# Linear attention and an MLP on one core: the keys' sum partly on VectorE, more warming matmuls, two denominators side by side, a new order

## The chip, the cores and the metric

The kernel runs on one core of a Trainium2 chip. The metric is device time in microseconds (us). Each run is one launch; the time before is the median of three.

## The reference

One transformer block with 2048 tokens of width 512 in bf16. What is computed, cut to the core:

```python
def _A_ref(x, wqkv, wo):                      # H = 32 heads of 16
    q, k, v = split(x @ wqkv)                 # each (heads, 2048, 16)
    phi = lambda t: jnp.where(t > 0, t + 1, jnp.exp(t)) + 1e-6
    pq, pk = phi(q), phi(k)
    kv  = jnp.einsum("bhsd,bhse->bhde", pk, v)
    z   = jnp.einsum("bhsd->bhd", pk)         # the keys' sum over all tokens
    num = jnp.einsum("bhqd,bhde->bhqe", pq, kv)
    den = jnp.einsum("bhqd,bhd->bhq", pq, z)[..., None] + 1e-6
    return merge_heads(num / den) @ wo
h  = x + _A_ref(_layernorm(x), A_wqkv, A_wo)
h2 = h + relu(_layernorm(h) @ B_w1) @ B_w2    # hidden width 1792
```

The second input `B_x` is not used.

## The kernel before

The tokens are 16 tiles of 128 rows (t = 0 to 15), and four chunks of 512 rows (c = 0 to 3); the width is four blocks of 128 columns (jb or kd = 0 to 3). All data stays on the chip. PSUM is one tile `bk` of eight banks, and the program assigns each bank by number.

The whole program is one string, `ORDER`. Each word is an operation with its indices: `K.8.0` calls `op_K(8, 0)`. The words are issued one after the other, and each goes to the queue of its engine, so on each engine the order of the words is the order of execution; semaphores between the engines follow from the tiles that are read and written. Nothing is reordered by a scheduler. An index list ends in a bank (TensorE), or in a count of neighbouring blocks (the others). All DMAs are issued by SyncE, in the order of the string, and a transposing DMA waits on that queue for its data.

The stages, with the words that the change and the prediction speak of:

- **Start.** `warm` issues matmuls of zeros into a bank that nobody reads (L233). `lx`, `lk`, `lq`, `lv`, `lo`, `l1`, `l2` load x and the weights wk, wq, wv, wo, w1, w2. For each tile `S` and `A` take mean and variance (VectorE, L236 and L237), `R` takes the reciprocal root as Ln and Exp (ScalarE, L242 and L243), `N` writes the normalised rows (VectorE, L250). They are transposed for tiles 0 to 5 on TensorE (`T`, L269) and copied out of PSUM by ScalarE or VectorE (`E`, `V`), and for tiles 6 to 15 by a transposing DMA (`X`, L290).
- **Keys.** `K` is x @ wk for a tile (four matmuls of 512 columns, L298). phi is Exp (`F`, ScalarE, L316), Relu (`U`, ScalarE, L319), min with 1 (`M`, VectorE, L323) and the sum of both (`D`, VectorE, L326). The keys lie in `pk`: tiles 0 and 1 in `pk_lo`, tile t from 2 on in slice t - 2 of `acts[0]`. `G` adds the outer product of normalised rows and keys for a tile into banks 4 to 7 (four matmuls, L350). `z` sums the keys over all tokens as matmuls of one column against ones (L358), one word for each block of 128 columns.
- **Attention's small matrices.** `gD` and `gA` copy G, `zc` and `zh` copy the keys' sum and spread it over heads, `kv`, `kx` and `m`, `mD` fold v's weights and wo into `m_sb`.
- **Queries.** `Q` (L306), `qF`, `qU`, `qM`, `qD` as for the keys, by chunk, into `pqT`.
- **Denominators.** `d4` gives the 32 heads' denominators for a chunk: four matmuls, each into 32 rows of one bank (L405). `dl4` and `dx4` make the reciprocals as Ln and Exp (ScalarE, L411 and L416) in `ld` and `rd`, which have two slots (c % 2). For chunk 0, `rp` spreads them by a matmul and `rm` multiplies; for the others `wb` writes them to DRAM, eight `rb` read them back spread over rows (L436), and `dm` multiplies (L443).
- **Second half.** `h` and `hD` give the attention's output plus x (L452, L458), `s`, `a`, `r`, `n` its layer norm, `t` or a DMA `x` its transposes, `p` (`ph` for half a chunk) the first layer of the MLP (L467, L476), `pA` and `pD` its Relu, `f` the second layer (L496), `fo` the result (L504) and `fd` its store.

The tile of zeros for the warming matmuls is a block of `m_sb`:

```python
zeros = m_sb[:, 0, :]
nc.vector.memset(zeros, 0.0)
```

Of the kernel before, what the change touches and what calls it, by code (L numbers as in the profile page):

```python
# [15 lines left out]


ORDER = """
table const masks warm.70.7.64 lx.0.1 S.0 lx.3.1 lx.2.1 lx.1.1 S.3 S.2 A.0 A.3 A.2 R.0.1 S.1 R.2.2 N.0.2.2 A.1
N.0.0.2 N.2 R.1.1 N.3 N.1 lk.0.2 lx.4.2 lk.2.2 T.0.3.2.2 warm.1.7 T.0.0.0.2 T.2.2 E.0.2.2 T.3.3 T.1.1 V.2  # L20
E.0.0.2 E.1 K.0.0 lx.6.2 S.4 E.3 S.5 A.5 A.4 F.0.1 R.4.2 U.0.1 S.7 S.6 M.0.1 N.4 K.2.2 K.1.1 F.1.1 U.1.1 K.3.3
D.0.1 A.6 A.7 R.6.2 M.1.1 N.5 lx.8.4 D.1.1 N.7 T.4.0 G.0 T.5.1 F.2.1 E.4 E.5 U.2.1 S.9 S.8 N.6 M.2.1 A.9 A.8
D.2.1 F.3.1 R.8.2 U.3.1 G.1 K.4.0 K.5.1 F.4.2 U.4.2 M.3.1 S.10 N.8 D.3.1 A.10 S.11 M.4.2 N.9 D.4.2 A.11
lx.12.4 lq.2.2 X.7 X.6 lv.0.2 R.10.2 G.2 K.7.3 G.3 K.6.2 F.6.2 U.6.2 lq.0.2 X.8 X.9 S.13 S.12 A.13 N.11 N.10
A.12 M.6.2 X.11 X.10 D.6.2 R.12.2 G.4 G.5 K.8.0 K.9.1 F.8.2 U.8.2 N.13 S.14 N.12 S.15 A.14 A.15 M.8.2 D.8.2
R.14.2 N.15 N.14 G.6 G.7 K.11.3 K.10.2 X.13 X.12 lo.2.2 X.14 X.15 l1.2.2 l2.0.7 lo.0.2 l1.0.2 lv.2.2 l2.7.7
F.10.2 U.10.2 G.8 G.9 K.12.0 K.13.1 U.12.2 F.12.2 M.10.2 D.10.2 M.12.2 G.10 K.14.2 K.15.3 Q.0.0.0 Q.0.1.1 G.11
F.14.2 U.14.2 M.14.2 D.12.2 G.12 D.14.2 qF.0.0.2 qU.0.0.2 G.13 z.1.2 G.14 Q.0.3.1 z.0.2 Q.0.2.0 G.15 z.2.2
z.3.2 qU.0.2.2 qF.0.2.2 gD.0.2 zc gA.2.2 qM.0.0.2 Q.1.1.3 Q.1.0.2 qF.1.0.2 qU.1.0.2 kv.1.4 kv.0.4 kv.3.4
kv.2.4 zh qM.0.2.2 qD.0.0.2 qD.0.2.2 kx Q.1.2.0 m.0.4 m.1.5 d4.0.3 m.3.7 m.2.6 Q.1.3.1 dl4.0 dx4.0 Q.2.1.3  # L30
qF.1.2.2 qU.1.2.2 qM.1.0.2 mD.0.2 mD.2.2 rp.0.0.4 rp.0.3.7 rp.0.1.5 rp.0.2.6 Q.2.0.2 qM.1.2.2 rm.0.0.2
rm.0.2.2 qD.1.0.2 qD.1.2.2 Q.2.3.1 Q.2.2.0 qU.2.0.2 qF.2.0.2 h.0.4 h.1.5 Q.3.0.2 Q.3.1.3 hD.0 hD.1 s.0 s.1 a.0
h.2.6 a.1 n.0 n.1 hD.2 qF.2.2.2 qU.2.2.2 h.3.7 t.0.4 qU.3.0.2 qF.3.0.2 e.0 Q.3.2.0 d4.1.4 t.1.5 Q.3.3.1 hD.3
s.2 s.3 a.2 a.3 n.2 n.3 v.1 t.2.6 dl4.1 dx4.1 qF.3.2.2 qU.3.2.2 v.2 t.3.7 wb.1 ph.0.1.3.0 ph.0.0.2.0 rb.1.0
rb.1.4 rb.1.2 rb.1.6 rb.1.1 rb.1.7 rb.1.5 rb.1.3 v.3 ph.0.1.3.1 ph.0.0.2.1 pD.0.0.2 qM.2.2.2 ph.0.3.1.1
ph.0.2.0.0 ph.0.2.0.1 ph.0.3.1.0 p.0.4.2 p.0.5.3 pA.0.2.2 p.0.6.0 p.0.7.1 pA.0.6.2 pD.0.4.2 p.0.8.2 p.0.9.3
p.0.11.1 p.0.10.0 pA.0.8.2 dm.1.0.2 dm.1.2.2 h.6.6 hD.6 h.5.5 p.0.13.3 h.7.7 hD.5 qM.3.0.2 s.6 a.6 s.5
qM.2.0.2 n.6 a.5 qD.2.2.2 h.4.4 hD.4 f.2.6.0.7 p.0.12.2 s.4 qD.2.0.2 qD.3.0.2 qM.3.2.2 hD.7 a.4 n.5 s.7 a.7
pA.0.10.2 pA.0.12.2 r.0.4 n.7 n.4 f.0.4.0.7 f.0.4.7.7 f.2.6.7.7 f.3.7.0.7 fo.0 x.5 x.4 x.6 fd.0 d4.2.4 dl4.2
dx4.2 x.7 wb.2 f.1.5.0.7 f.3.7.7.7 f.1.5.7.7 p.1.1.1 p.1.0.0 p.1.2.2 p.1.3.3 rb.2.6 rb.2.0 rb.2.4 rb.2.2  # L40
rb.2.7 rb.2.5 rb.2.3 rb.2.1 fo.3 pA.1.0.2 fo.1 fo.2 pA.1.2.2 dm.2.2.2 dm.2.0.2 p.1.4.0 p.1.5.1 p.1.6.2 p.1.7.3
r.4.4 pA.1.4.2 p.1.8.0 p.1.9.1 h.11.7 h.10.6 h.8.4 pD.1.8.2 pA.1.6.2 p.1.10.2 p.1.13.1 p.1.11.3 pA.1.10.2 hD.8
s.8 hD.11 h.9.5 p.1.12.0 f.4.4.0.7 pA.1.12.2 hD.10 s.10 f.4.4.7.7 f.7.7.0.7 hD.9 s.11 a.11 s.9 a.9 n.11 n.9
a.8 a.10 n.10 qD.3.2.2 fo.4 n.8 x.11 x.9 x.8 x.10 d4.3.4 dl4.3 dx4.3 wb.3 fd.1 f.6.6.0.7 f.5.5.0.7 f.6.6.7.7
p.2.0.0 p.2.3.3 p.2.2.2 p.2.1.1 pA.2.0.2 pD.2.2.2 fd.3 rb.3.6 rb.3.0 rb.3.7 rb.3.4 rb.3.2 rb.3.1 rb.3.5 rb.3.3
fd.4 fd.2 f.5.5.7.7 p.2.4.0 f.7.7.7.7 fo.5 p.2.7.3 p.2.6.2 p.2.5.1 pA.2.4.2 dm.3.2.2 fo.7 dm.3.0.2 h.12.4
h.13.5 hD.12 fo.6 pA.2.6.2 p.2.9.1 p.2.10.2 p.2.8.0 pD.2.8.2 r.8.4 p.2.11.3 h.15.7 p.2.12.0 p.2.13.1 pA.2.12.2
pA.2.10.2 h.14.6 f.8.4.0.7 s.12 hD.15 hD.13 s.13 a.13 hD.14 f.10.6.0.7 a.12 n.13 n.12 s.14 a.14 s.15 a.15 n.15
n.14 fd.5 fd.6 x.12 x.15 f.11.7.0.7 f.8.4.7.7 f.9.5.0.7 f.10.6.7.7 fo.8 fd.7 x.14 x.13 f.11.7.7.7 f.9.5.7.7
p.3.1.1 p.3.0.0 pA.3.0.2 p.3.2.2 p.3.3.3 p.3.5.1 p.3.4.0 fo.9 pA.3.4.2 fo.11 pD.3.2.2 fo.10 p.3.7.3 p.3.6.2  # L50
p.3.9.1 p.3.8.0 pD.3.6.2 pD.3.8.2 f.14.6.0.7 f.13.5.0.7 p.3.13.1 p.3.10.2 p.3.12.0 p.3.11.3 pA.3.12.2 r.12.4
pD.3.10.2 f.12.4.0.7 f.14.6.7.7 f.13.5.7.7 f.12.4.7.7 fd.10 fd.8 fd.9 fd.11 fo.13 fo.14 fo.12 fd.12 fd.14
fd.13 f.15.7.0.14.0.2 fo.15.0.2 fd.15.0.2 f.15.5.0.14.3.1 fo.15.3.1 fd.15.3.1 f.15.4.0.14.2.1 fo.15.2.1
fd.15.2.1
"""


# [1 line left out]
def kernel(  # L59
# [94 lines left out]
    def pk(t, n=1):  # L154
        return pk_lo[:, t : t + n, :] if t < 2 else acts[0][:, t - 2 : t - 2 + n, :]
# [22 lines left out]
        )  # L178

    def op_const():  # L180
        nc.vector.memset(zeros, 0.0)
# [2 lines left out]
        nc.vector.memset(ones[:], 1.0)
# [23 lines left out]
    def op_masks():  # L208
        op_mask()
        op_maskh()  # L210


    def op_gate():
        nc.gpsimd.memset(wk_sb[:, 0:4:2, 0:1], 0.0)
# [133 lines left out]
    def op_G(t):  # L348
        for kd in range(KD):
# [2 lines left out]
                start=(t == 0), stop=(t == NT - 1),  # L352
            )

    def op_z(jb, b):
        at_bank["z"] = b
        for t in range(NT):
            nc.tensor.matmul(  # L358
                bk[:, b, jb : jb + 1], lhsT=pk(t)[:, 0, jb * P : (jb + 1) * P], rhs=ones[:],
                start=(t == 0), stop=(t == NT - 1),  # L360
            )
# [37 lines left out]

    def op_d4(c, b):
        at_bank["d4", c] = b
        for jb in range(KD):
            nc.tensor.matmul(  # L405
                bk[jb * Q4 : (jb + 1) * Q4, b, :], lhsT=zhd[:, jb, :], rhs=pqT[c][:, jb, :],
                start=True, stop=True,
            )
# [138 lines left out]
```

## Time and profile before

| | us |
|---|---|
| runs | 173.38, 173.40, 173.82 |
| median | 173.40 |
| profiled execution | 173.59 |
| its span in the profile | 171.9 |
| TensorE busy / VectorE / ScalarE | 166.4 / 94.8 / 66.2 |
| first transpose on TensorE | 5.96 |
| keys of tile 8 begin on TensorE | 22.25 |

The span runs from the first recorded instruction to the last; the rest of an execution's time lies around it. In the rows of the profile PE is TensorE's matmuls, PEld its weight loads, DVE VectorE, ACT ScalarE, POOL GpSimd, SP SyncE. L298 is line 298 of the kernel. A row of the groups ends with the busy time, the mean length in ns, and the idle time ahead with what ended it. Matmul ends are modelled, so lengths of matmuls are read here from one start to the next. The clock column (1.00 throughout) is the share of the full TensorE clock that the throttle granted.

### The profile page before, as it was taken

What the parts mean: (1) busy time and instruction counts of PE and PEld (TensorE: products, weight loads), DVE (VectorE), ACT (ScalarE), POOL (GpSimd) and SP (SyncE); (2) the same over time, 40 slices, a digit from 0 to 9 for tenths busy, and PEclk for the clock granted to TensorE, in tenths of its full rate; (3) what the DMA queues carried; (4) which work ended last, traced back from release to release, by engine and by line L of the source; (5) the groups of instructions that cost most, each with busy time, mean ns of one, the idle gap of its engine ahead of it and who ended that gap; (6) DMA issues with size and microseconds to landing.
All of it is one profiled execution on the core that took longest, in us unless ns stands there. A gap on an engine that the chain in (4) does not pass through costs nothing.

```text
span 171.9 us, 2470 instructions
## 1 busy us (share of the span) xinstructions
PE 166.4 (97%) x963; PEld 81.9 (48%) x963; DVE 94.8 (55%) x198; ACT 66.2 (39%) x98; POOL 4.7 (3%) x21
## 2 busy tenths in 40 slices
...
GB/s 132 293 250 61 184 93 123 244 373 367 26 6 0 0 60 97 0 0 0 98 104 103 4 2 0 95 146 158 34 31 0 39 114 0 0 126 0 0 0 122
DMA packets 22619, 14.97 MB, mean 87 GB/s; under 512 B 13264, under 2 KB 21584, under 8 KB 22608
## 3 DMA queue, kind: packets, MB, share of 16 engines
...
q8 instruction: 7, 0.11, 0.3%
...
## 4 chain that ended last, share of the span: by engine, by line
PE 89%; DMA 4%; ACT 3%; DVE 2%; issue 0%
PE bk L496 28%; PE bk L467 26%; PE bk L306 8%; PE bk L452 8%; PE bk L298 6%; PE bk L350 5%; DMA lnT<-h_nat 3%; PE bk L476 2%; PE bk L269 2%; DVE st L236 2%; DMA x_nat<-in_A_x_dram 1%; ACT eb L316 1%; PE bk L358 1%; ACT rb L319 1%; PE bk L405 1%; PE bk L392 1%
## 5 line engine op out<-in xcount | busy, mean ns | idle before, releaser
L496 PE MATMUL bk<-w_sb,at 128*128 128x512 bf16 (+2 forms) x252 | 50.1, 355 | 0.0
L467 PE MATMUL bk<-lnT,w_sb 128*128 128x512 bf16 x208 | 47.0, 379 | 0.0
L482 ACT ACTIVATE at<-bk 128x1024 bf16<-128x1024 f32 x19 | 19.2, 1023 | 65.7 <-PE bk L467 63.6
L496 PEld LDWEIGHTS <-at 128*128 128x128 bf16 x252 | 23.4, 98 | 25.1 <-issue 0.5
L467 PEld LDWEIGHTS <-w_sb 128*128 128x128 bf16 x208 | 20.3, 98 | 24.3
L487 DVE TENSOR_SCALAR at<-bk 128x1024 bf16<-128x1024 f32 x9 | 11.0, 1225 | 24.6 <-PE bk L467 23.2
L504 DVE SCALAR_TENSOR_TENSOR gT<-bk,rstd,h_nat 128x512 bf16<-128x512 f32 (+2 forms) x18 | 12.2, 689 | 20.1 <-PE bk L496 16.5
L319 ACT ACTIVATE rb<-bk 128x1024 bf16<-128x1024 f32 (+1 forms) x18 | 16.7, 927 | 7.1 <-PE bk L306 5.6
L316 ACT ACTIVATE eb<-bk 128x1024 bf16<-128x1024 f32 (+1 forms) x18 | 16.6, 928 | 5.0 <-PE bk L298 4.5
L298 PE MATMUL bk<-wk_sb,lnT 128*128 128x512 bf16 x64 | 16.0, 395 | 0.6 <-DMA lnT<-h_nat 0.6
L306 PE MATMUL bk<-lnT,wq_sb 128*128 128x512 bf16 x64 | 15.5, 379 | 0.0
L452 PE MATMUL bk<-m_sb,pqs 128*128 128x512 bf16 x64 | 15.3, 379 | 0.0
L458 DVE TENSOR_TENSOR h_nat<-bk,x_nat 128x512 bf16<-128x512 f32 x16 | 10.8, 686 | 6.7 <-PE bk L452 6.5
L350 PE MATMUL bk<-at,h_nat 128*128 128x512 bf16 x56 | 13.6, 379 | 0.0
L236 DVE BATCH_NORM_STATS2 st<-x_nat 128x6 f32<-128x512 bf16 x16 | 10.3, 678 | 2.0 <-DMA x_nat<-in_A_x_dram 2.0
L238 DVE BATCH_NORM_STATS2 st<-h_nat 128x6 f32<-128x512 bf16 x16 | 10.7, 682 | 0.1
L298 PEld LDWEIGHTS <-lnT 128*128 128x128 bf16 x64 | 6.4, 102 | 8.8 <-DMA lnT<-h_nat 1.1
L323 DVE TENSOR_SCALAR eb<-eb 128x1024 bf16<-128x1024 bf16 (+1 forms) x18 | 7.0, 389 | 6.5 <-ACT eb L316 6.5
L452 PEld LDWEIGHTS <-pqs 128*128 128x128 bf16 x64 | 6.3, 98 | 7.5
L350 PEld LDWEIGHTS <-h_nat 128*128 128x128 bf16 x64 | 6.1, 98 | 6.8
L306 PEld LDWEIGHTS <-wq_sb 128*128 128x128 bf16 x64 | 5.9, 97 | 6.4 <-issue 0.2
L443 DVE TENSOR_TENSOR pqs<-pqT,rr 128x1024 bf16<-128x1024 bf16 x6 | 4.0, 688 | 5.5 <-DMA rr<-scr 5.3
...
## 6 DMA issues: line engine op xcount, KB each, us to landing
...
```

Of the source, the lines that this page charges most:

```text
L236: op_S = lambda t: nc.vector.bn_stats(out=st[:, t, :], in_=x_nat[:, t, :])
L298: nc.tensor.matmul(bk[:, b, :], lhsT=lnT[c][:, kd, j * P : (j + 1) * P], rhs=wk_sb[:, kd, :], start=(kd == 0), stop=(kd == KD - 1),)
L306: nc.tensor.matmul(bk[:, b, :], lhsT=wq_sb[:, kd, j * P : (j + 1) * P], rhs=lnT[c][:, kd, :], start=(kd == 0), stop=(kd == KD - 1),)
L316: nc.scalar.activation(out=buf(eb, kind, i, n), in_=bank(at_bank[kind, i], n), func=ACT.Exp)
L319: nc.scalar.activation(out=buf(rb, kind, i, n), in_=bank(at_bank[kind, i], n), func=ACT.Relu)
L350: nc.tensor.matmul(bk[:, KD + kd, :], lhsT=ln_nat[:, t, kd * P : (kd + 1) * P], rhs=pk(t)[:, 0, :], start=(t == 0), stop=(t == NT - 1),)
L452: nc.tensor.matmul(bk[:, b, :], lhsT=pqs[:, (c * KD + jb) % NQ, j * P : (j + 1) * P], rhs=m_sb[:, jb, :], start=(jb == 0), stop=(jb == KD ...
L467: nc.tensor.matmul(bk[:, b, :], lhsT=w1_sb[:, kd, f * P : (f + 1) * P], rhs=lnT[c][:, kd, :], start=(kd == 0), stop=(kd == KD - 1),)
L482: nc.scalar.activation(out=acts[c % 2][:, f : f + n, :], in_=bank(at_bank["p", c, f], n), func=ACT.Relu)
L487: nc.vector.tensor_scalar(out=acts[c % 2][:, f : f + n, :], in0=bank(at_bank["p", c, f], n), scalar1=0.0, scalar2=None, op0=ALU.max,)
L496: nc.tensor.matmul(bk[:, b, 0 : w * P], lhsT=acts[c % 2][:, f, j * P : (j + 1) * P], rhs=w2_sb[:, f, k * P : (k + w) * P], start=(f == 0), ...
L504: nc.vector.scalar_tensor_tensor(out=o_t[:, t % NO, cols], in0=bk[:, at_bank["f", t, k], 0 : w * P], scalar=rstd2[:, t : t + 1], in1=h_nat ...
```

## The change

- **The keys' sum.** `op_zr(j, n)` sums the keys of tiles 2 to 13 (the 12 slices of `acts[0]`, `ZT`) for one block of 128 columns on VectorE, reading through a view in which the tile is the inner index, so that neighbouring reads are 512 bf16 elements apart. `op_zhi` rounds the f32 sums to bf16 and `op_zlo` keeps the remainder. `op_z` then multiplies these two rows and the keys of tiles 0, 1, 14 and 15 with ones: 6 matmuls a block instead of 16.
- **Warming.** The string gets `warm.2.7` (two matmuls of 512 columns) behind the 70 small ones, and `warm.1.7` moves from between the halves of tile 0's transposes to the place ahead of them. The memset of the zeros is made in two parts, 128 columns first.
- **Denominators.** `op_d4` takes a count: `d4.2.0.2` makes those of chunks 2 and 3, one after the other in banks 0 and 1. `ld` and `rd` get a slot for each chunk.
- **The order** is a new one throughout. Among much else: x tiles load as 3, 1, 0, 2; half of wo loads ahead of the x tiles 8 to 15, and lv and lq, which stood ahead of `X.8`, come behind `X.13`; `zr` of three blocks stands ahead of `M.14` and `D.14`, and the last with `zhi` and `zlo` behind them; `gD` stands ahead of `zc`.
- Functions without a word in the string are taken out (`op_gate`, `op_lkA`).

```diff
-table const masks warm.70.7.64 lx.0.1 S.0 lx.3.1 lx.2.1 lx.1.1 S.3 S.2 A.0 A.3 A.2 R.0.1 S.1 R.2.2 N.0.2.2 A.1
-N.0.0.2 N.2 R.1.1 N.3 N.1 lk.0.2 lx.4.2 lk.2.2 T.0.3.2.2 warm.1.7 T.0.0.0.2 T.2.2 E.0.2.2 T.3.3 T.1.1 V.2
...
-F.14.2 U.14.2 M.14.2 D.12.2 G.12 D.14.2 qF.0.0.2 qU.0.0.2 G.13 z.1.2 G.14 Q.0.3.1 z.0.2 Q.0.2.0 G.15 z.2.2
-z.3.2 qU.0.2.2 qF.0.2.2 gD.0.2 zc gA.2.2 qM.0.0.2 Q.1.1.3 Q.1.0.2 qF.1.0.2 qU.1.0.2 kv.1.4 kv.0.4 kv.3.4
...
+table const masks warm.70.7.64 warm.2.7 lx.3.1 S.3 lx.1.1 S.1 lx.0.1 S.0 lx.2.1 A.1 A.0 S.2 lk.0.2 lx.4.2
+lk.2.2 lx.6.2 R.0.1 R.1.1 A.3 A.2 N.0.0.2 N.0.2.2 N.1 R.2.2 N.2 warm.1.7 T.0.3.2.2 T.0.0.0.2 T.1.1 T.2.2
+E.0.2.2 E.0.0.2 N.3 S.4 S.5 V.2 A.4 A.5 S.6 S.7 T.3.3 E.1 E.3 K.0.0 K.1.1 K.2.2 K.3.3 F.0.1 R.4.2 U.0.1 F.1.1
+M.0.1 A.6 A.7 R.6.2 U.1.1 lo.2.2 lx.8.4 lq.2.2 lx.12.4 N.4 D.0.1 M.1.1 N.6 N.5 X.6 T.4.0 G.0 T.5.1 E.4 U.2.1
...
+N.9 A.10 D.3.1 A.11 U.4.2 F.4.2 R.10.2 S.12 M.4.2 N.11 D.4.2 S.13 N.10 A.13 A.12 X.8 K.7.3 K.6.2 G.3 K.8.0
+F.6.2 U.6.2 R.12.2 X.9 M.6.2 N.12 N.13 D.6.2 S.15 S.14 A.15 A.14 G.4 X.11 K.9.1 G.5 K.11.3 X.10 X.12 X.13
+F.8.2 U.8.2 R.14.2 G.6 K.10.2 F.10.2 U.10.2 N.14 N.15 M.8.2 M.10.2 D.8.2 K.12.0 K.13.1 F.12.2 M.12.2 D.10.2
+U.12.2 D.12.2 lv.2.2 lq.0.2 X.14 X.15 l1.2.2 l1.0.2 l2.7.7 lv.0.2 lo.0.2 l2.0.7 G.7 G.8 G.9 Q.0.0.0 K.14.2
+K.15.3 Q.0.1.1 G.10 G.11 F.14.2 U.14.2 qF.0.0.2 qU.0.0.2 G.12 zr.1.1 zr.2.1 zr.0.1 M.14.2 D.14.2 zr.3.1 zhi
+zlo G.13 Q.0.3.1 G.14 Q.0.2.0 G.15 z.1.2 z.2.2 z.3.2 z.0.2 gD.0.2 zc qF.0.2.2 gA.2.2 qU.0.2.2 Q.1.1.3 Q.1.0.2
+kv.0.4 kv.1.4 kv.2.4 kv.3.4 qM.0.0.2 zh qD.0.0.2 qM.0.2.2 qD.0.2.2 kx qF.1.0.2 qU.1.0.2 qM.1.0.2 Q.1.2.0 m.0.4
...
+    ZT = 12
...
+    zacc = big.tile([P, D], F32, name="zacc")
+    zhl = big.tile([P, 2, D], BF16, name="zhl")
...
-    ld = big.tile([P, 2, CW], F32, name="ld")
-    rd = big.tile([P, 2, CW], BF16, name="rd")
+    ld = big.tile([P, NCH, CW], F32, name="ld")
+    rd = big.tile([P, NCH, CW], BF16, name="rd")
...
-        nc.vector.memset(zeros, 0.0)
+        nc.vector.memset(zeros[:, 0:P], 0.0)
...
+        nc.vector.memset(zeros[:, P:], 0.0)
...
+    def op_zr(j, n):
+        cols = slice(j * P, (j + n) * P)
+        nc.vector.tensor_reduce(
+            out=zacc[:, cols], in_=acts[0][:, 0:ZT, cols].rearrange("p t n -> p n t"),
+            op=ALU.add, axis=mybir.AxisListType.X,
+        )
+
+    def op_zhi():
+        nc.vector.tensor_copy(out=zhl[:, 0, :], in_=zacc[:])
+
+    def op_zlo():
+        nc.vector.tensor_tensor(out=zhl[:, 1, :], in0=zacc[:], in1=zhl[:, 0, :], op=ALU.subtract)
+
     def op_z(jb, b):
         at_bank["z"] = b
-        for t in range(NT):
+        parts = [zhl[:, i, :] for i in range(2)] + [pk(t)[:, 0, :] for t in range(NT) if not 2 <= t < ZT + 2]
+        for i, part in enumerate(parts):
             nc.tensor.matmul(
-                bk[:, b, jb : jb + 1], lhsT=pk(t)[:, 0, jb * P : (jb + 1) * P], rhs=ones[:],
-                start=(t == 0), stop=(t == NT - 1),
+                bk[:, b, jb : jb + 1], lhsT=part[:, jb * P : (jb + 1) * P], rhs=ones[:],
+                start=(i == 0), stop=(i == len(parts) - 1),
             )
...
-    def op_d4(c, b):
-        at_bank["d4", c] = b
-        for jb in range(KD):
...
+    def op_d4(c0, b0, n=1):
+        for c, b in zip(range(c0, c0 + n), range(b0, b0 + n)):
+            at_bank["d4", c] = b
+            for jb in range(KD):
...
-            out=ld[:, c % 2, :], in_=bk[:, at_bank["d4", c], :], func=ACT.Ln, bias=eps6[:], scale=1.0
+            out=ld[:, c, :], in_=bk[:, at_bank["d4", c], :], func=ACT.Ln, bias=eps6[:], scale=1.0
```

More of the change, by code (lines that the diff above doesn't have):

```diff
@@ L18 @@
 ORDER = """
-table const masks warm.70.7.64 lx.0.1 S.0 lx.3.1 lx.2.1 lx.1.1 S.3 S.2 A.0 A.3 A.2 R.0.1 S.1 R.2.2 N.0.2.2 A.1
-N.0.0.2 N.2 R.1.1 N.3 N.1 lk.0.2 lx.4.2 lk.2.2 T.0.3.2.2 warm.1.7 T.0.0.0.2 T.2.2 E.0.2.2 T.3.3 T.1.1 V.2
-E.0.0.2 E.1 K.0.0 lx.6.2 S.4 E.3 S.5 A.5 A.4 F.0.1 R.4.2 U.0.1 S.7 S.6 M.0.1 N.4 K.2.2 K.1.1 F.1.1 U.1.1 K.3.3
-D.0.1 A.6 A.7 R.6.2 M.1.1 N.5 lx.8.4 D.1.1 N.7 T.4.0 G.0 T.5.1 F.2.1 E.4 E.5 U.2.1 S.9 S.8 N.6 M.2.1 A.9 A.8
-D.2.1 F.3.1 R.8.2 U.3.1 G.1 K.4.0 K.5.1 F.4.2 U.4.2 M.3.1 S.10 N.8 D.3.1 A.10 S.11 M.4.2 N.9 D.4.2 A.11
@@ L24 @@
[L24 to L27, printed above, removed]
-F.14.2 U.14.2 M.14.2 D.12.2 G.12 D.14.2 qF.0.0.2 qU.0.0.2 G.13 z.1.2 G.14 Q.0.3.1 z.0.2 Q.0.2.0 G.15 z.2.2
@@ L29 @@
-z.3.2 qU.0.2.2 qF.0.2.2 gD.0.2 zc gA.2.2 qM.0.0.2 Q.1.1.3 Q.1.0.2 qF.1.0.2 qU.1.0.2 kv.1.4 kv.0.4 kv.3.4
[L30 to L53, printed above, removed]
@@ L54 @@
-fd.15.2.1
+table const masks warm.70.7.64 warm.2.7 lx.3.1 S.3 lx.1.1 S.1 lx.0.1 S.0 lx.2.1 A.1 A.0 S.2 lk.0.2 lx.4.2
+lk.2.2 lx.6.2 R.0.1 R.1.1 A.3 A.2 N.0.0.2 N.0.2.2 N.1 R.2.2 N.2 warm.1.7 T.0.3.2.2 T.0.0.0.2 T.1.1 T.2.2
+E.0.2.2 E.0.0.2 N.3 S.4 S.5 V.2 A.4 A.5 S.6 S.7 T.3.3 E.1 E.3 K.0.0 K.1.1 K.2.2 K.3.3 F.0.1 R.4.2 U.0.1 F.1.1
+M.0.1 A.6 A.7 R.6.2 U.1.1 lo.2.2 lx.8.4 lq.2.2 lx.12.4 N.4 D.0.1 M.1.1 N.6 N.5 X.6 T.4.0 G.0 T.5.1 E.4 U.2.1
+E.5 F.2.1 N.7 D.1.1 K.4.0 G.1 K.5.1 S.8 S.9 M.2.1 X.7 A.9 A.8 U.3.1 R.8.2 F.3.1 D.2.1 S.11 G.2 N.8 S.10 M.3.1
@@ new lines @@
+zlo G.13 Q.0.3.1 G.14 Q.0.2.0 G.15 z.1.2 z.2.2 z.3.2 z.0.2 gD.0.2 zc qF.0.2.2 gA.2.2 qU.0.2.2 Q.1.1.3 Q.1.0.2
+kv.0.4 kv.1.4 kv.2.4 kv.3.4 qM.0.0.2 zh qD.0.0.2 qM.0.2.2 qD.0.2.2 kx qF.1.0.2 qU.1.0.2 qM.1.0.2 Q.1.2.0 m.0.4
+m.1.5 d4.0.3 m.3.7 m.2.6 Q.1.3.1 dl4.0 dx4.0 qF.1.2.2 qU.1.2.2 mD.0.2 mD.2.2 Q.2.1.3 rp.0.1.5 rp.0.3.7
+rp.0.2.6 rp.0.0.4 Q.2.0.2 Q.2.3.1 Q.2.2.0 qD.1.0.2 rm.0.0.2 rm.0.2.2 qM.1.2.2 qD.1.2.2 h.0.4 hD.0 s.0 a.0
+h.3.7 h.1.5 h.2.6 n.0 t.0.4 qF.2.0.2 qU.2.0.2 qU.2.2.2 qF.2.2.2 e.0 Q.3.1.3 d4.1.4 Q.3.0.2 dl4.1 dx4.1
@@ new lines @@
+qU.3.0.2 qF.3.0.2 wb.1 rb.1.2 rb.1.6 rb.1.0 rb.1.4 rb.1.3 rb.1.1 rb.1.7 rb.1.5 hD.1 hD.3 hD.2 s.1 s.3 a.1 a.3
+n.1 s.2 n.3 a.2 n.2 Q.3.3.1 t.1.5 Q.3.2.0 qU.3.2.2 qF.3.2.2 t.3.7 t.2.6 v.1 ph.0.1.3.0 ph.0.0.2.0 v.3 v.2
+ph.0.1.3.1 ph.0.0.2.1 qM.3.0.2 qM.2.2.2 pD.0.0.2 dm.1.2.2 dm.1.0.2 ph.0.2.0.1 ph.0.2.0.0 ph.0.3.1.0 ph.0.3.1.1
+p.0.4.2 p.0.5.3 pA.0.2.2 p.0.6.0 p.0.7.1 qD.3.0.2 pA.0.4.2 qM.3.2.2 p.0.8.2 p.0.9.3 h.5.5 h.7.7 h.6.6 pA.0.6.2
+pA.0.8.2 p.0.12.2 h.4.4 p.0.10.0 qM.2.0.2 hD.5 hD.7 s.5 hD.4 a.5 s.4 hD.6 n.5 s.6 s.7 a.6 a.4 n.4 a.7 qD.3.2.2
@@ new lines @@
+qD.2.0.2 n.7 qD.2.2.2 n.6 p.0.11.1 f.3.7.0.7 f.1.5.0.7 r.0.4 pA.0.10.2 p.0.13.3 f.2.6.0.7 d4.2.0.2 pA.0.12.2
+dl4.3 dl4.2 x.5 x.4 x.7 x.6 f.0.4.0.7 f.2.6.7.7 p.1.0.0 p.1.3.3 p.1.2.2 p.1.1.1 f.1.5.7.7 pD.1.2.2 dx4.3 dx4.2
+pA.1.0.2 p.1.5.1 f.0.4.7.7 f.3.7.7.7 wb.2 rb.2.6 wb.3 rb.2.0 rb.2.2 rb.2.4 p.1.4.0 pA.1.4.2 p.1.6.2 p.1.7.3
+p.1.9.1 p.1.8.0 fo.0 fo.1 rb.2.3 rb.2.1 rb.2.5 rb.2.7 pA.1.6.2 fo.2 dm.2.2.2 dm.2.0.2 pA.1.8.2 fo.3 h.10.6
+h.11.7 hD.11 h.8.4 hD.8 hD.10 s.10 p.1.13.1 h.9.5 f.4.4.0.7 p.1.10.2 p.1.12.0 a.10 s.11 hD.9 s.9 a.11 n.11 a.9
@@ new lines @@
+p.1.11.3 f.6.6.0.7 pD.1.12.2 r.4.4 pA.1.10.2 rb.3.2 rb.3.6 fd.3 fd.0 fd.1 rb.3.0 rb.3.4 n.10 n.9 s.8 a.8 n.8
+rb.3.7 rb.3.1 rb.3.3 x.10 x.9 x.8 x.11 f.7.7.0.7 f.5.5.0.7 f.4.4.7.7 f.5.5.7.7 f.6.6.7.7 f.7.7.7.7 p.2.3.3
+fd.2 rb.3.5 dm.3.2.2 fo.4 dm.3.0.2 fo.7 fo.6 p.2.0.0 p.2.2.2 pD.2.2.2 h.12.4 h.14.6 p.2.6.2 p.2.1.1 hD.12 fo.5
+p.2.7.3 h.15.7 hD.15 pA.2.0.2 r.8.4 p.2.4.0 p.2.5.1 h.13.5 pA.2.6.2 pA.2.4.2 p.2.10.2 p.2.11.3 s.12 s.15 a.15
+hD.13 hD.14 n.15 p.2.8.0 f.9.5.0.7 p.2.9.1 fd.5 fd.4 s.14 s.13 pA.2.8.2 a.12 a.13 n.12 a.14 n.14 n.13
@@ new lines @@
+f.10.6.0.7 p.2.13.1 p.2.12.0 x.15 x.12 fd.6 x.14 fd.7 x.13 pA.2.12.2 pA.2.10.2 f.8.4.0.7 f.11.7.0.7 f.9.5.7.7
+p.3.0.0 f.11.7.7.7 f.8.4.7.7 p.3.1.1 p.3.2.2 p.3.3.3 pA.3.0.2 fo.8 fo.11 pD.3.2.2 p.3.5.1 p.3.4.0 f.10.6.7.7
+p.3.6.2 p.3.7.3 pA.3.4.2 p.3.9.1 p.3.8.0 fo.10 pA.3.6.2 fo.9 p.3.10.2 f.13.5.0.7 p.3.11.3 pD.3.10.2 pA.3.8.2
+p.3.12.0 p.3.13.1 pA.3.12.2 r.12.4 f.14.6.0.7 f.12.4.0.7 f.12.4.7.7 f.13.5.7.7 fd.11 fd.9 fd.8 fd.10 fo.13
+f.14.6.7.7 fo.14 fo.12 fd.13 fd.12 f.15.5.0.14.3.1 fo.15.3.1 fd.14 fd.15.3.1 f.15.7.0.14.0.2 fo.15.0.2
@@ L55 @@
+fd.15.0.2 f.15.4.0.14.2.1 fo.15.2.1 fd.15.2.1
 """
```

26 lines of the change are left out of this document (9 added, 17 removed).

## The prediction

> **What bounds the kernel now.** I read the page first, then TensorE's waits, the chain that ended last, the groups by form, and the busy time by stage.
>
> ```profile
> span 171.9 us, 2470 instructions
> PE 166.4 (97%) x963; PEld 81.9 (48%) x963; DVE 94.8 (55%) x198; ACT 66.2 (39%) x98; POOL 4.7 (3%) x21
> ```
>
> TensorE is busy 97%, VectorE 55%. TensorE's waits are three, all in the first 22.3 us:
>
> ```profile
> PE bk L233 <- DVE ones L184: 1.3, 1, 1.3
> PE bk L269 <- DVE h_nat L250: 0.8, 1, 0.8
> PE bk L298 <- DMA lnT<-h_nat: 0.6, 1, 0.6
> ```
>
> From the chain (start, length, what):
>
> ```profile
> 5.96 0.39 PE bk L269 x2
> 6.36 0.43 PE bk L233
> 6.78 1.49 PE bk L269 x14
> 8.28 3.41 PE bk L298 x12
> ...
> 17.63 4.58 DMA lnT<-h_nat
> 22.20 0.05 issue
> 22.25 1.90 PE bk L298 x8
> 24.15 1.73 PE bk L350 x8
> ...
> 37.97 0.38 PE bk L358 x16
> ```
>
> Eight 512-wide matmuls take 1.73 us, 216 ns each, from 24 us to the end; from 22.25 on the chain is nearly all TensorE, back to back. So behind 22.25 time is gained by taking matmuls away, and lost by any late operand. Ahead of it two things show: 14 transposes took 1.49 us (106 ns each, 56 ns later on), and 12 matmuls 3.41 us, which is four at 427 ns and eight at 216. The array ran at half rate until 9.77, although the clock column reads full. And tile 8's transposed rows landed after 4.58 us, where the median of these transposes is 2.5; by the starts in the timeline TensorE lost 0.80 there (the next matmul was due at 21.45).
>
> **Fewer matmuls for the keys' sum.** `op_z` went through 16 tiles for each of four column blocks; now through two summed rows and four tiles: 64 matmuls become 24. A set of 16 takes 0.38 to 0.40 us, 25 ns each: 40 x 25 ns = **-1.0 us**.
>
> **The strided sums.** Four `op_zr` of 128 outputs x 12 inputs, `op_zhi` (512 f32 to bf16) and `op_zlo` (512, f32) go to VectorE. No row shows a reduction. The nearest rows:
>
> ```profile
> L487 DVE TENSOR_SCALAR at<-bk 128x1024 bf16<-128x1024 f32 x9 | 11.0, 1225 | 24.6 <-PE bk L467 23.2 <-PE bk L476 1.4
> L388 DVE TENSOR_TENSOR kvbd<-bk,mask 128x512 bf16<-128x512 f32 x1 | 0.7, 692 | 0.4 <-PE bk L380 0.4
> L326 DVE TENSOR_TENSOR at<-rb,eb 128x1024 bf16<-128x1024 bf16 x6 | 4.0, 688 | 1.2 <-ACT rb L319 1.2
> L288 DVE COPY lnT<-bk 128x512 bf16<-128x512 bf16 x3 | 1.1, 414 | 0.0
> ```
>
> From 692 to 1225 ns for 512 more elements is 1.04 ns an element, 0.16 fixed: 1536 elements are 1.76 us, some 1.67 behind another instruction (VectorE starts the next about 0.09 before one ends, by pairs in the timeline). The low end is L326's two elements per cycle, 0.95 us. The high end is no row's: these reads step 1 KB between elements, which no instruction here does; two cycles for each would be 3.4 us. I take 1.7, since the slope of every one-at-a-time VectorE row is 1.04, and keep both ends. `op_zhi` about 0.5 (between L288 and L388), `op_zlo` 0.69.
>
> Is there room? In the new order TensorE runs sixteen sets of four matmuls from K.13 up to the first z (K.13, G.7 to G.9, Q, K.14, K.15, Q, G.10 to G.13, Q, G.14, Q, G.15): 16 x 0.863 = 13.8 us. VectorE can begin the sums when D.12 is done: 1.03 for K.13's result, 0.2 behind U.10 on ScalarE, 1.02 and 0.92 for F.12 and U.12, 0.7 for D.12, 3.9 in all. Of the 9.9 left, M.14 and D.14 take 1.1, `op_zhi` and `op_zlo` with their hand-overs 1.2, leaving 7.6: four sums at **1.9 us** each just fit, and at 1.7 they end 0.8 early. M.14 and D.14 stand behind three sums on VectorE, and G.14 waits for D.14: G.14 is 13 sets (11.2 us) after K.13, which allows 2.08 a sum. So the sums cost nothing, and the cover is VectorE's idle time in these stages (behind the comma stand PE, PEld, then DVE, each with its count):
>
> ```profile
> 30.00:35.00 5.00, 5.00 (x25) 2.26 (x24) 0.99 (x3) 3.25 (x4) 0.00 (x0) 1.00 0.80 251
> 35.00:40.00 5.00, 5.00 (x41) 2.52 (x40) 1.37 (x3) 2.46 (x3) 0.00 (x0) 1.00 1.07 385
> ```
>
> Past 1.9, every 0.1 us in a sum is 0.4 us on the path: z, `zc`, `zh`, d4 and all behind them wait.
>
> **Denominators of chunks 2 and 3 together.** A d4 of four matmuls takes 0.33 in the chain, and the 21 matmuls behind it 4.64 instead of 4.53: 0.44 for one that stands alone. As a pair the second four still stream 512 columns through the same four column groups, at least 0.22. **-0.2** (between 0 and -0.4). Ln and Exp of both fall where ScalarE had waited 4.9 us for d4; `ld` and `rd` have a slot per chunk now, so nothing is overwritten early.
>
> **The start.** The 70 small warming matmuls end at 4.98 and the first transposes start at 5.96, a gap of 0.98. Two of 512 columns (0.43 each at half rate) and the single one, moved ahead of the transposes, make 1.28: the gap almost closes. Tile 0 is now third to load, so `N.0` comes behind four `S` and four `A`: 2.98 + 4 x 0.66 + 4 x 0.06 = 5.9, plus two half-tiles of 0.3: first transposes at about 6.4, 0.45 later. They then follow the `N` at 0.33 each, and K.0 starts at about 7.55 (before: 8.07). Before, 3.8 us of work since 5.96 brought the clock up at 9.77; counted from 1.25 without a gap it is up well ahead of K.0, whose four matmuls then take 0.86 instead of 1.71. K of tiles 0 to 3 would end at 11.0 instead of 12.37. Next late is `N.4`: VectorE now has S.6 and S.7 ahead of it, and they wait for a load that landed at 9.56. 9.59 + S.6, S.7, M.0, A.6, A.7, N.4 (0.6 + 0.6 + 0.2 + 0.1 + 0.1 + 0.4) is 11.6, and D.0 for G.0 0.1 more. **-0.7**, not -1.4.
>
> [...]
>
> **Tile 8's wait.** The loads lv.0 and lq.0 (landed 19.46 and 20.20) lay just ahead of X.8 on SyncE's queue; now they come behind X.13. X.8 follows N.8 at about 16.1; at 2.5 it lands at 18.6, and K.8, which no longer has G.4 and G.5 ahead, is due at 19.0. **-0.8**, with 0.4 us of margin. wo's half has moved ahead of the last x loads, which costs those about 1 us; their readers S.8 to S.13 come later than that. lv and lq now lie ahead of X.14 and X.15, as they did of X.8 (4.6 us): 25.3 + 4.6 = 29.9, K.14 due at 30.3.
>
> **New small waits.** `zc` now stands behind the 1.23 us of `gD`, and Q.1.0 needs its bank (0.1); kvbd comes behind two more adds (0.1); two hidden-layer halves need banks that chunk 3's Exp, now behind its Relu, frees last (0.1 each). **+0.3** after taking off the like waits of before. Behind 62 us the order keeps TensorE's set of matmuls, and I find no operand less than 0.2 us early.
>
> Sum: -1.0 - 0.2 - 0.7 - 0.8 + 0.3 = **-2.4**. The profiled execution took 173.59 (span 171.9 and 1.7 around it): **171.2**. The median of the runs is 173.40, 0.2 lower, well inside my uncertainty.
>
> **Rivals.** *Slow strided reads (slower).* For: no row has such a step, and the whole cover is 0.2 us a sum. Against: every row's slope is 1.04 ns. From 1.9 us a sum on, four times the excess is lost. At one and a half cycles an element a sum is 1536 x 1.56 + 0.16 = 2.56: +2.6, 173.8. At two, 3.35: +5.8, 177.0. TensorE would then wait at G.14 (for D.14's add) and at the first z, VectorE being busy without a break from D.12 to `zlo`. [...]
>
> *A start that is not gained.* The clock comes up at 9.8 again, because the small matmuls don't count or the phase is unlucky: four or so matmuls at half rate, 0.8 back: 172.0. Or a transpose of tiles 7, 8 or 13 (margins 0.3 to 0.5) lands 1 us late under the moved loads: up to 172.8. Against: 22 us later all is loaded, and six transposes in a row, from tile 11 on, took 2.4 to 2.5.
>
> *The filling matmuls do not do what they say*: the gap closes but the array was waiting for `N` anyway. Without the clock it is the case just priced.
>
> **Numbers.** Sums at row speed and the start gained: 0.39, 170.5 to 171.9. Start not gained: 0.12, to 172.8. Reads at about one and a half cycles: 0.25, 173.0 to 174.8. Two cycles or more: 0.19, 175 to 177. Something unseen that loses: 0.05. Faster by over 0.3% (0.5 us, about what a measurement of this kernel can tell from none): 0.39 + 0.12 + 0.02 = 0.53; within: 0.08, from the third case; slower: 0.15 + 0.19 + 0.05 = 0.39. The range from 170.5 to 175.6 leaves out most of the two-cycle case. The likeliest case alone is 170.5 to 171.9.
>
> **What would show it.** Right: a TENSOR_REDUCE row of 1.65 to 1.8 us x4, no TensorE wait between 22 and 40 us, transposes at 56 ns, K.0 in 0.86 us, z sets of 0.15 us. Wrong: a mean above 2.0 in that row, with waits of G's matmuls on the add and of z's on `zhl`; or K.0 at 427 ns a matmul; or a wait on lnT's transposes.

## The result, and the profile after

The changed kernel is 0.7% slower: 173.95 us median over 12 runs (173.73 to 174.38), against 173.07 for the kernel before over 12 runs (171.78 to 173.82; the three on record before are among them). The ratio is 1.0074, with a 95% interval of 1.005 to 1.0099. Forecast were 171.2, with a range of 170.5 to 175.6: the time lies inside the range, but it moved the other way.

The profiled run took 173.75 (span 172.0). Its page, and TensorE's waits in total, count and longest one:

```profile
span 172.0 us, 2380 instructions
PE 163.7 (95%) x909; PEld 80.0 (47%) x925; DVE 102.0 (59%) x202; ACT 68.9 (40%) x101; POOL 4.7 (3%) x21
```

```profile
PE bk L343 <- DVE at L319: 1.9, 1, 1.9
PE bk L226 <- DVE m_sb L184: 1.0, 1, 1.0
PE bk L262 <- DVE h_nat L243: 0.9, 1, 0.9
PE bk L366 <- DVE zhl L360: 0.5, 1, 0.5
PE bk L366 <- DVE zhl L357: 0.4, 1, 0.4
```

TensorE has 2.7 us less work by this count and takes as long. (Sixteen matmuls are missing from the trace, 909 against 925 weight loads, so the 2.7 may be too high.) The wait for tile 8's transpose is gone, and three new ones name VectorE: G (L343) waits for the keys' add (L319), and z (L366) for the rounded sums and their remainder. The group of the strided sums says why (the row ends with busy time, mean ns of one, idle time ahead):

```profile
L351 DVE TENSOR_REDUCE zacc<-at 128x128 f32<-128x1536 bf16 x4 | 10.9, 2779 | 0.0
```

A sum takes 2.78 us, not 1.7. The timeline (start, length, what) shows the queue that this makes:

```profile
29.39 8.16 DVE L351 TENSOR_REDUCE zacc<-at 128x128 f32<-128x1536 bf16 x3
37.99 0.69 DVE L319 TENSOR_TENSOR at<-rb,eb 128x1024 bf16<-128x1024 bf16 x1
38.60 2.78 DVE L351 TENSOR_REDUCE zacc<-at 128x128 f32<-128x1536 bf16 x1
38.74 1.02 PE L343 MATMUL bk<-at,h_nat 128*128 128x512 bf16 x4 [1.85 <-DVE at L319]
...
41.90 0.18 PE L366 MATMUL bk<-ones,zhl 128*128 128x1 bf16 x1 [0.41 <-DVE zhl L357]
42.62 0.18 PE L366 MATMUL bk<-ones,zhl 128*128 128x1 bf16 x1 [0.55 <-DVE zhl L360]
```

Three sums hold VectorE for 8.16 us from 29.39. `M.14` and `D.14` stand behind them in VectorE's order, so `D.14` ends at 38.7 and G.14 starts there, 2.0 us after its due time (the four matmuls before it, from 35.86, have streamed by 36.73). The fourth sum, `zhi` and `zlo` run on to 42.6. G.15's four matmuls are through at 41.3, and z, which needs both rows, gets its second at 42.62: another 1.28.

The start did what was forecast, and a little more:

```profile
6.56 1.37 PE L262 MATMUL bk<-ident,h_nat 128*128 128x128 bf16 x16 [0.88 <-DVE h_nat L243]
7.76 3.62 PE L291 MATMUL bk<-wk_sb,lnT 128*128 128x512 bf16 x16
```

Sixteen transposes fit into 1.2 us, and sixteen matmuls of the first keys into 3.46 (both from start to start), where they took 2.11 (with a warming matmul among them) and 4.31 before.

The two profiles balance when the same work is compared by its start on TensorE. At G.13 the changed kernel is 1.94 ahead (35.00 against 36.94); the waits for the sums take 2.01 and 1.28 of it, the shorter z gives 1.0 back, and at Q.1.1.3 it is 0.35 behind. The pair of denominators gives 0.22: its second four matmuls add 0.22 to the first, where a set that stood alone cost 0.44. The last matmul starts 0.14 later than before (169.01 against 168.87), and the run is 0.16 longer. So on these two profiles the change ends level. The 0.88 between the medians has a second cause, the spread of the launches of the kernel before, which profiles of it show further down.

### The profile page after: what moved, and what is told of

Read it like the earlier page. It is cut to its first block, busy times and chain, and to the rows that moved or that the text cites. A ratio compares the mean times of both kernels' runs of the same rounds, so it can differ in the third digit from the quotient of the medians.

```text
span 172.0 us, 2380 instructions
## 1 busy us (share of the span) xinstructions
PE 163.7 (95%) x909; PEld 80.0 (47%) x925; DVE 102.0 (59%) x202; ACT 68.9 (40%) x101; POOL 4.7 (3%) x21
## 4 chain that ended last, share of the span: by engine, by line
PE 73%; DVE 19%; ACT 3%; DMA 1%; issue 1%; another core or an unknown queue 0%; DVEq 0%
PE bk L505 28%; PE bk L476 26%; PE bk L461 8%; DVE zacc L351 6%; PE bk L299 6%; DVE st L229 5%; DVE h_nat L243 3%; PE bk L485 2%; DVE at L319 2%; DMA x_nat<-in_A_x_dram 1%; ACT eb L309 1%; ACT rb L312 1%; DVE eb L316 1%; DVE mv L230 1%; PE bk L414 1%
## 5 line engine op out<-in xcount | busy, mean ns | idle before, releaser
L491 ACT ACTIVATE at<-bk 128x1024 bf16<-128x1024 f32 x22 | 22.4, 1022 | 69.8 <-PE bk L476 62.5
L476 PE MATMUL bk<-lnT,w_sb 128*128 128x512 bf16 x201 | 47.5, 379 | 0.3
L496 DVE TENSOR_SCALAR at<-bk 128x1024 bf16<-128x1024 f32 x6 | 7.3, 1224 | 14.8 <-PE bk L476 14.2
L343 PE MATMUL bk<-at,h_nat 128*128 128x512 bf16 x55 | 13.5, 379 | 1.9 <-DVE at L319 1.9
L291 PE MATMUL bk<-wk_sb,lnT 128*128 128x512 bf16 x63 | 15.2, 379 | 0.1
L351 DVE TENSOR_REDUCE zacc<-at 128x128 f32<-128x1536 bf16 x4 | 10.9, 2779 | 0.0
L343 PEld LDWEIGHTS <-h_nat 128*128 128x128 bf16 x64 | 6.2, 98 | 9.3 <-issue 2.1
```

The lines of the kernel that those rows point to most:

```text
L291: nc.tensor.matmul(bk[:, b, :], lhsT=lnT[c][:, kd, j * P : (j + 1) * P], rhs=wk_sb[:, kd, :], start=(kd == 0), stop=(kd == KD - 1),)
L343: nc.tensor.matmul(bk[:, KD + kd, :], lhsT=ln_nat[:, t, kd * P : (kd + 1) * P], rhs=pk(t)[:, 0, :], start=(t == 0), stop=(t == NT - 1),)
L351: nc.vector.tensor_reduce(out=zacc[:, cols], in_=acts[0][:, 0:ZT, cols].rearrange("p t n -> p n t"), op=ALU.add, axis=mybir.AxisListType.X,)
L476: nc.tensor.matmul(bk[:, b, :], lhsT=w1_sb[:, kd, f * P : (f + 1) * P], rhs=lnT[c][:, kd, :], start=(kd == 0), stop=(kd == KD - 1),)
L491: nc.scalar.activation(out=acts[c % 2][:, f : f + n, :], in_=bank(at_bank["p", c, f], n), func=ACT.Relu)
```

## The experiments

My theory for them: the strided sums are the whole loss, their reads cost 1.6 times what the rows of neighbouring reads said, and the rest of the change gains. The rivals: another part of the new order loses, or the sums' place in VectorE's order loses, whatever they take. Each expectation below names its own rivals beside these.

**The same sums over neighbouring elements.** Each sum reads 1536 neighbouring elements in groups of 12; the sums are then of other elements than the reference's.

```
-  in_=acts[0][:, 0:ZT, cols].rearrange("p t n -> p n t"),
+  in_=acts[0][:, 3*j : 3*j+3, :].rearrange("p t d -> p (t d)").rearrange("p (n i) -> p n i", i=ZT),
```

> The changed kernel with each of the four VectorE sums reading 1536 neighbouring elements, in place of 128 columns of 12 tiles (the sums are then of other elements); count, order, outputs and waits stay. Theory (a step of 1 KB between reads makes a sum 2.78 us, and what it takes beyond 1.95 us, four times, is lost): a sum 1.6 to 1.8 us, TensorE's waits ahead of G.14 (2.0) and the z matmuls (1.3) gone, time 3.3 below the changed kernel: 170.7. Rival A (a reduction in groups of 12 is slow whatever the step): sums stay above 2.5 us and the time within 0.5 of 173.95. Rival B (the sums are slowed by the traffic of those stages, not by their step): the same as A.

Measured: 170.44 us (170.19 to 170.83), 0.9869 of the kernel before (0.9831 to 0.9907). The group:

```profile
L351 DVE TENSOR_REDUCE zacc<-at 128x128 f32<-128x1536 bf16 x4 | 6.8, 1743 | 0.0
```

Same instruction, same elements in number, same place: 1.74 us in place of 2.78, and no wait of TensorE at G.14 or z. That is 3.5 us off the changed kernel's time with nothing moved, by the medians and by the ratios alike. Both rivals of the expectation fall, and so does the rival that the place in VectorE's order loses whatever the sums take. The 1.7 of the prediction was right for these reads, and wrong for those that the change makes.

**No sums at all.** `zr`, `zhi` and `zlo` are left out, and z goes through 16 tiles as before.

```
-G.12 zr.1.1 zr.2.1 zr.0.1 M.14.2 D.14.2 zr.3.1 zhi zlo G.13
+G.12 M.14.2 D.14.2 G.13
```

> The changed kernel without the VectorE sums: z goes through 16 tiles on TensorE as before the change, everything else in the new order. Theory: the stall of 3.3 goes, 40 matmuls of 25 ns (1.0) come back: 171.6 to 171.7. This prices the rest of the change (start, tile 8's transpose, denominators, order) at about -1.4 against the median before (173.07). Rival A (the new order has lost something besides the sums): 172.5 or more.

Measured: 171.69 (171.25 to 172.44), 0.9944 of before (0.9916 to 0.9971). Against the changed kernel that is 2.26 less, where 3.29 of waits less 1.0 of z make 2.29. Against the kernel with cheap sums, run on the same chip, it is 1.25 more, of which z's 40 matmuls are 1.0. The rival of this expectation falls. But all else in the change gains 0.8 of a typical run of before, where I expected 1.4, and not the 2.2 (1.94 and 0.22) that the two profiles show. The kernels that follow, up to the one with the loads put back, bear on that difference.

**The kernel before with the gap filled.** `warm.2.7` added behind the 70 small matmuls of the kernel before, nothing else.

```
-table const masks warm.70.7.64 lx.0.1
+table const masks warm.70.7.64 warm.2.7 lx.0.1
```

> The kernel before with two more warming matmuls of 512 columns behind the 70 small ones, nothing else. Theory (the runs before lie between 171.8 and 173.8 because the array's clock comes up at about 5 us in some launches and at 9.8 in others, by what the gap of 0.98 leaves): without the gap all runs lie at 171.8 to 172.2, K.0 at 216 ns a matmul. Rival (the spread comes from tile 8's transposing DMA): K.0 is fast and the runs are spread over 171.8 to 173.8 as they were.

Measured: 172.32 median, 0.9977 of before (0.9947 to 1.0007); ten of its runs lie between 171.82 and 172.53, one at 173.4, and one of 986.92 is left out. I had expected all of them at 172.2 or less. Long times became rarer (one of eleven above 172.6, ten of 23 for the kernel before beside it), but the median hardly moves, because about half of those runs of before (171.71 to 173.88) lay in that range already. In the profile K.0 ran at 216 ns a matmul; but the rate doubled at 4.3, while the 70 small matmuls still ran and ahead of the two added ones, so this launch does not show that they brought it about.

**The kernel before, profiled again**, three times in all, unchanged.

> The kernel before, unchanged, for a second profile. Theory (clock): if this execution takes 172.3 or less, K.0 runs at 216 ns a matmul; if 173 or more, at 427. Rival (transpose): K.0 at 427 in either, and the landing of tile 8's rows decides.

> The kernel before, unchanged, once more for its profile. Two profiles of it had the clock up at 9.6 to 9.8 us, K.0 at 427 ns a matmul and times of 173.6 and 173.0, while its runs spread from 171.6 to 173.9. Theory (the spread is the clock's rise together with the landing of tile 8's transpose): a profile of 172.2 or less shows K.0 at 216 ns or K.8 begun by 21.5 on the trace's axis, one of 172.8 or more shows neither. Rival (the spread lies elsewhere): a profile of 172.2 or less with K.0 cold and K.8 at 21.6 or later, the difference lying behind 24 us.

> The kernel before, unchanged, a second copy for its profile; expected as for the other copy: at 172.2 or less the clock up early or tile 8's keys begun by 21.5, at 172.8 or more neither; the rival has the difference behind 24 us.

Measured: 172.98, 173.46 and 172.11. In the last of them the timeline has the keys of the first tiles, and then those of tile 8:

```profile
6.32 1.68 PE L269 MATMUL bk<-ident,h_nat 128*128 128x128 bf16 x16 [1.16 <-DVE h_nat L250]
7.84 3.62 PE L298 MATMUL bk<-wk_sb,lnT 128*128 128x512 bf16 x16
...
20.79 1.90 PE L298 MATMUL bk<-wk_sb,lnT 128*128 128x512 bf16 x8 [0.25 <-ACT rb L319]
```

In the run of 173.46:

```profile
8.06 4.49 PE L298 MATMUL bk<-wk_sb,lnT 128*128 128x512 bf16 x16
...
22.13 1.90 PE L298 MATMUL bk<-wk_sb,lnT 128*128 128x512 bf16 x8 [0.50 <-DMA lnT<-h_nat]
```

And in that of 172.98:

```profile
21.62 1.90 PE L298 MATMUL bk<-wk_sb,lnT 128*128 128x512 bf16 x8 [0.21 <-DMA lnT<-h_nat]
```

Take the start of K.8 from the run's time, for the four profiles of this kernel: 173.59 - 22.25 = 151.34, 173.46 - 22.13 = 151.33, 172.98 - 21.62 = 151.36, 172.11 - 20.79 = 151.32. All of the spread lies ahead of tile 8's keys; behind them the kernel takes the same time within 0.04. In the run of 172.11 the transposes and K.0 ran at full rate from 6.3 on, though the gap ahead of them was 1.3 us; in the three others K.0 ran at 427 ns a matmul and the rate doubled between 9.4 and 9.8. The theory holds and the rival (a difference behind 24 us) falls. The kernel before has launches with an early and a late clock, and my prediction was worked out against a late one. (A clock that comes up stands here for what the trace shows, matmuls of 512 columns 427 ns apart and then 216; the clock column itself reads 1.00 over the whole start of the kernel before, in a late launch.)

**No sums, with less filling.** First `warm.2.7` alone is taken away, then `warm.1.7` as well.

```
-table const masks warm.70.7.64 warm.2.7 lx.3.1
+table const masks warm.70.7.64 lx.3.1
...
-N.2 warm.1.7 T.0.3.2.2
+N.2 T.0.3.2.2
```

> The kernel without VectorE sums (171.69) less its two extra warming matmuls of 512 columns. Theory of the clock (70 small ones, 3.7 us, are too short to bring it up in most launches; 4.6 us do): K.0 at 427 ns a matmul in the profile, up to 0.8 longer ahead of N.4's wait of which 0.3 to 0.8 stays: 172.0 to 172.5, with more spread. Rival (what follows N.4 hides the whole of it): 171.5 to 171.9.

Measured: 171.54 (171.16 to 172.78), 0.9963 of before (0.9931 to 0.9996). A miss: I expected a late clock and 172.0 to 172.5. Nine of twelve runs lie at 171.85 or lower, three near 172.7; the profiled run, 171.24, had the clock up by 6.33 without the two matmuls.

> The kernel without the sums, and also without the three filling matmuls ahead of the transposes (only the 70 small ones are left). It prices the filling wholly, beside the kernel without the sums (171.69 us over 12 runs) and the one that kept only the single matmul (171.54). Theory (the filling is worth what the clock is worth): with a gap of over 1 us ahead of the first transposes the clock comes up at about 9.6 as in the kernel before, K.0 runs at 427 ns a matmul, and the time is 172.0 to 172.5 (0.8 back, of which some is hidden behind the wait for N.4). Rival (the clock's rise is not set by these three matmuls): K.0 at 216 ns, transposes at 56 ns, and a median within 0.3 of 171.6.

Measured: 172.75 (171.47 to 174.11), 0.9968 of before (0.9942 to 0.9994); the profiled run took 172.98. Its transposes and the first keys:

```profile
6.35 1.89 PE L262 MATMUL bk<-ident,h_nat 128*128 128x128 bf16 x16 [1.39 <-DVE h_nat L243]
8.04 0.63 PE L291 MATMUL bk<-wk_sb,lnT 128*128 128x512 bf16 x1
```

The transposes are 107 ns apart again, K.0's matmuls 427, and the rate doubles between 9.3 and 9.7; tile 4's transposes start at 12.54, and at 11.42 in the kernel with all three. In this launch the clock was late, as the theory has it, and the median lies above its 172.0 to 172.5: the loss is 1.06 by the medians. But this kernel ran on another chip, where before took 172.91; by the ratios it is 0.4. What the filling is worth on a typical launch stays open between these two.

**The loads ahead of X.8 put back.** No sums, and `lv.2.2 lq.0.2` in front of `X.8` as in the kernel before.

```
-A.13 A.12 X.8 K.7.3
+A.13 A.12 lv.2.2 lq.0.2 X.8 K.7.3
...
-D.12.2 lv.2.2 lq.0.2 X.14 X.15
+D.12.2 X.14 X.15
```

> The kernel without VectorE sums (171.69) with the loads of half of wv and half of wq issued ahead of tile 8's transposing DMA, as they were before the change. Theory (those two loads held tile 8's rows up): the transpose takes 4.1 to 4.6 us in place of 2.4, lands at about 19.7 where K.8 is due at 18.8, and TensorE waits 0.7 to 1.1 there: 172.4 to 172.8. Rival (the loads do not matter, the lateness before came from the order of VectorE's work): landing at 17.8 to 18, time 171.5 to 171.9.

Measured: 171.73 (171.58 to 172.59), 0.9965 of before (0.9937 to 0.9993), where the kernel without the move has 0.9944 on another chip. A miss: I expected 172.4 to 172.8. X.8 took 3.2 us from its issue to its landing in place of 2.4. It was issued at 15.7, where the kernel before issues it at 17.6, and landed at 18.96. The timeline has G.3, then K.8's matmuls and their weight loads:

```profile
17.75 1.03 PE L343 MATMUL bk<-at,h_nat 128*128 128x512 bf16 x4
19.00 1.04 PE L291 MATMUL bk<-wk_sb,lnT 128*128 128x512 bf16 x4 [0.23 <-ACT eb L309]
19.00 0.55 PEld L291 LDWEIGHTS <-lnT 128*128 128x128 bf16 x4 [0.72 <-DMA lnT<-h_nat]
```

G.3's four matmuls have streamed by 18.62, so K.8 began 0.38 late. The matmuls' row puts the wait down to ScalarE's Exp, which ended at 18.98, the row of the weight loads to the transposed rows. It is the rows: without the move K.8 began at 18.78, while the same Exp ran from 18.12 to 19.14. The loads cost the transpose 0.8 us and TensorE about 0.4, half of the 0.80 that the kernel before lost there; medians taken on two chips cannot tell so little. The other half of the lost wait goes with the rest of the new order, which issues X.8 two microseconds sooner. That was read from the traces, not tried by itself, and why the same two loads went with 2.1 us more for the transpose in the kernel before and 0.8 here stays open.

**The reduction by its step.** One kernel reads 1536 neighbouring elements in four orders, with steps between the reads of 4, 8, 2 and 64 elements; the sums are of other elements than the reference's.

```
+  s = (2, 4, 8, 64)[j]
+  in_=acts[0][:, 3*j : 3*j+3, :].rearrange("p t d -> p (t d)").rearrange("p (m i s) -> p m s i", i=ZT, s=s),
```

> The changed kernel with its four VectorE sums reading a block of 1536 neighbouring elements in another order each: the inner 12 reads step by 2, 4, 8 and 64 bf16 elements (blocks 0 to 3; the sums are of other elements). Measured so far: step 1 is 1.74 us, step 512 is 2.78 us. Theory (a read that opens a new short piece of memory each time costs about 0.65 of a cycle more, however far it goes): step 64 at 2.7 to 2.8 us, step 8 (16 bytes) the same or near it, steps 2 and 4 (4 and 8 bytes) in between or at 1.74. Rival (the price grows with the distance, or is one of rows 1 KB apart): step 64 well below 2.7, steps 2 to 8 at 1.74.

Measured: 171.46 in one run. The timeline of the four sums, with steps of 4, 8, 2 and 64 elements:

```profile
29.03 1.75 DVE L352 TENSOR_REDUCE zacc<-at 128x128 f32<-128x1536 bf16 x1
```

```profile
30.70 2.92 DVE L352 TENSOR_REDUCE zacc<-at 128x128 f32<-128x1536 bf16 x1
```

```profile
33.53 1.75 DVE L352 TENSOR_REDUCE zacc<-at 128x128 f32<-128x1536 bf16 x1
```

```profile
36.32 2.79 DVE L352 TENSOR_REDUCE zacc<-at 128x128 f32<-128x1536 bf16 x1
```

With the two kernels above the row of steps is: 2 bytes 1.74 us, 4 bytes 1.75, 8 bytes 1.75, 16 bytes 2.92, 128 bytes 2.79, 1 KB 2.78. The price, 1.0 to 1.2 us in 1536 reads, comes at once between 8 and 16 bytes and does not grow with distance, up to 1 KB. Why it comes there the runs do not show.

**The same sums by whole-row additions.** Four VectorE additions take the place of the four reductions: six tiles onto six, three onto three, and two of one tile. All reads are of neighbouring elements.

```
-G.12 zr.1.1 zr.2.1 zr.0.1 M.14.2 D.14.2 zr.3.1 zhi zlo
+G.12 zt.0 zt.1 M.14.2 D.14.2 zt.2 zt.3 zhi zlo
...
+        out, in0, in1 = (
+            (zf[:, 0:6, :], src[:, 0:6, :], src[:, 6:12, :]),
+            (zf[:, 0:3, :], zf[:, 0:3, :], zf[:, 3:6, :]),
+            (zf[:, 0, :], zf[:, 0, :], zf[:, 1, :]),
+            (zacc[:], zf[:, 0, :], zf[:, 2, :]),
+        )[i]
+        nc.vector.tensor_tensor(out=out, in0=in0, in1=in1, op=ALU.add)
```

> The changed kernel with the keys of the 12 tiles summed by four VectorE additions of whole neighbouring rows in place of the four strided sums: 6 + 6 tiles (3072 elements, f32 out), 3 + 3 (1536), then 512 twice; the first two ahead of M.14 and D.14, the rest behind them. Theory (one element per cycle for reads side by side): 3.4, 1.8, 0.7 and 0.7 us, 6.4 in all against room for 7.6, TensorE's waits at G.14 and z gone: 170.4 to 170.8, as with the sums of neighbouring elements (170.44). Rival (VectorE work of this length in these stages delays something else, such as chunk 0's queries): 171 or more.

Measured: 170.37 (170.25 to 170.80), 0.9888 of before (0.9847 to 0.9929). VectorE's timeline:

```profile
29.35 5.15 DVE L359 TENSOR_TENSOR at<-at 128x3072 f32<-128x3072 bf16 x2
...
35.55 0.68 DVE L359 TENSOR_TENSOR at<-at 128x512 f32<-128x512 f32 x1
36.27 0.69 DVE L359 TENSOR_TENSOR zacc<-at 128x512 f32<-128x512 f32 x1
```

The four take 3.36 + 1.76 + 0.68 + 0.69 = 6.5 us in place of 11.1, `D.14` ends in time, and TensorE waits neither at G.14 nor at z. This version does what the change set out to do, and is faster than both kernels.

## Why the prediction was wrong, step by step

- **The strided sums are the step that failed.** I took 1.7 us a sum "since the slope of every one-at-a-time VectorE row is 1.04". Every row behind that slope reads neighbouring elements, so none could speak for a step of 1 KB; a sum measured 2.78. The price of an excess was right: four times 2.78 less the 3.29 lost leaves a cover of 1.96 a sum, between the two that I had given (1.9 for all four, 2.08 up to G.14), and it was lost at the two places named. The rival of slow strided reads is what happened, near the time worked out for one and a half cycles (173.8). That it is so near is in part luck: by that rival's own rule 2.78 a sum gives 171.2 + 4 x (2.78 - 1.9) = 174.7, and the start, the small waits and the cover came out 1.0 better than forecast. Per element, with the fixed 0.16 us of my estimate taken off, the strided sum took (2.78 - 0.16) / 1536 = 1.71 ns and the sum of neighbouring reads (1.74 - 0.16) / 1536 = 1.03. I had let rows that could not bear on the question settle it.
- **z**: 1.0 forecast, 1.0 found. **Denominators**: 0.2 forecast, 0.22 found.
- **The start, the clock and tile 8 together**: 1.5 forecast against the profiled run, 1.94 found against it. First transposes came at 6.56 (forecast 6.4), K.0 at 7.76 (7.55), K.0 in 0.86, and no wait for lnT. At tile 4's transposes the changed kernel is 1.16 ahead (11.22 against 12.38), where I had 0.7: `N.4` ended at 11.0, not at 11.6. The other 0.78 is tile 8, forecast 0.8; but the reason that I gave, the loads on the queue, accounts for only about half of it (0.38 of wait with the loads put back). The gap ahead of the transposes did not close either: TensorE waited 0.88 there. That 3.8 us of work brought the clock up was my reading of one launch, and no run shows what brings it up, the length of the work or a phase: in the same kernel the rise came at 9.77 in that launch, and ahead of the first transposes, in an idle gap of over 1 us, in the run of 172.11.
- **The base of that gain was wrong too.** I wrote that the median lay 0.2 below the profiled run, "well inside my uncertainty". The profiled run was a launch with a late clock, and by their times (173.38 to 173.82) so were the three runs at hand; later medians of the same kernel, on more than one chip, were 173.07, 172.5, 172.15 and 172.91. A launch whose clock comes up early leaves the new start 0.48 to gain by G.13 (by its weight loads: 35.26 in the run of 172.11, 34.78 in the changed kernel), not 1.94. This is why the two profiles are level and the medians are not: the changed kernel's runs hardly spread, those of before reach down to 171.6.
- **New small waits**: 0.3 forecast, about 0 found (0.35 behind at Q.1.1.3, less 0.22 for the pair, 0.14 at the last matmul).

Put in order, 171.2 + 3.3 for the sums - 0.44 for the start - 0.3 for the small waits is 173.76; the profiled run took 173.75.
